# One exponential fill moved from the long attention visit to the short one

## The chip, the cores and the metric

The kernel runs on one core of a Trainium2 chip. The metric is the device time of one execution in microseconds, the median of several runs; lower is better.

## The reference

The reference adds an attention with a compressive memory and a gated feed-forward network, each weighted by a gate that is computed from the input. Cut to what matters:

```python
B, S, D, H, N, F = 1, 2048, 640, 32, 4, 1728      # Dh = 20, L = S // N = 512
g = sigmoid((x * gate_w).sum(-1, keepdims=True))
q, k, v = (x @ wq, x @ wk, x @ wv)                # as (B, H, N, L, Dh)
for s in range(N):                                # segments of 512 rows
    logits = einsum("bhqd,bhkd->bhqk", qs, ks) * Dh ** -0.5 + causal_mask
    a_dot = softmax(logits) @ vs
    a_mem = (phi(qs) @ M) / (phi(qs) @ z + 1e-6)  # phi(t) = t + 1 if t > 0 else exp(t)
    outs.append(sigmoid(beta) * a_mem + (1 - sigmoid(beta)) * a_dot)
    M, z = M + phi(ks).T @ vs, z + phi(ks).sum(0)
a = concat(outs) @ wo
b = (silu(x @ w1) * (x @ w3)) @ w2
return g * a + (1 - g) * b
```

## The kernel before

The work has two strands that share the tensor engine. The dense strand holds the products with 128x128 weight blocks: the projections (tiles `q`, `k`, `v`), the feed-forward network (`g` and `u` up, `f` down) and the output projection (`op`). Each of these is a *fill*: 9 or 15 matmuls of 512 columns (5 for the last down group) that add up in one PSUM bank, which one or two operations on VectorE or ScalarE then read out. The attention strand works on *quads* of four heads of one segment; there are 32 heads in 4 segments, so 32 quads.

A quad needs five `s` fills, five `t` fills and one `o` fill. An `s` fill computes scores by rows for two heads, one bank each, and VectorE reduces them to row maxima (line L641: one reduction, and one read of its accumulator into tile `m`, for every block of 128 query rows). A `t` fill computes transposed scores with the maxima already subtracted, again one bank for each of two heads; ScalarE turns them into exponentials in tile `P` (L673), GpSimd zeroes the masked part (L677). The `o` fill multiplies `P` of all four heads with the values into one bank, which VectorE copies to tile `oq` (L691). Two heads stand in the upper and lower 64 rows of the tensor engine, so their matmuls run side by side.

The eight PSUM banks are given out in the order of a queue. `bank_tile` takes the bank at the head. A small tile (`s`, `t`, `o`, `rr`, `nd`, ...) goes back to the tail at once, so the next user of that bank comes eight tiles later and waits for its readers. A dense fill is `held`: its bank is out of the queue until `filled()` at its last matmul.

The order on the tensor engine is the order in which the code is run (`manual_schedule` for that engine); the other engines' orders are the framework's. The main loop runs two generators. `attention()` goes through rounds `m`, each of 40 slots `n`, and issues the attention work; `step` issues a few dense matmuls (three, mostly) and adds to a counter, `clock["step"]`. In every slot the dense strand is run for as long as its share of the time lasts. In round `m` two slots carry a *visit*, a row of attention fills without a dense matmul in between. The long one (`BIG`, slot 5) has the fills 0, 2 and 1 of `s` for quad `m`, four `t` fills for quad `m - 1` and the `o` fill for quad `m - 2`. The short one (`SMALL`, slot 17) has `s` fills 3 and 4 and `t` fill 4. Before a visit the loop takes up to four or eight more dense steps until a condition holds: the long visit wants no fill held, that is a place between two dense fills; the short one ("amid") wants the held fill to have come far enough, and stands in its midst.

After the short visit, `max_rows` prepares the maxima for the next round and `load_pair` fetches queries and keys by DMA from GpSimd's queue in slots 12 and 18.

Of the kernel before, what the change touches and what calls it, by code (L numbers as in the profile page):

```python
# [18 lines left out]
S, D, H, DH, NSEG, L = 2048, 640, 32, 20, 4, 512  # L19
# [6 lines left out]
BIG = -1.0e38  # L26
# [12 lines left out]
def gated_mix(ctx: ExitStack, tc: tile.TileContext, xT, wqk, wv, w13, w2, w2h, wo, beta, out):  # L39
# [60 lines left out]


    here = tc.keep_in_program_order
    last = {}

    def split(dst, src, lo=None, pin=lambda ins: ins):
        pin(nc.scalar.copy(dst[:, 0], src))  # L106
# [2 lines left out]
    free, held = list(range(NB)), {}  # L109

    def bank_tile(name, hold=None):


        k = free.pop(0)
        ps = pp.tile([P, L], F32, tag=f"b{k}", name=name, bufs=1)
        if hold:
            held[k] = -hold
        else:
            free.append(k)
        return ps  # L120
# [6 lines left out]
    def split_psum(dst, src, name, pin=lambda ins: ins):  # L127

        hi = bank_tile(name)[:, :src.shape[-1]]
        pin(nc.scalar.copy(dst[:, 0], src))  # L130
        nc.scalar.copy(hi, dst[:, 0].bitcast(F32))
        nc.vector.tensor_sub(dst[:, 1], src, hi)
# [7 lines left out]
    def big_tile(name, dt=F32):  # L140
        return sp.tile([P, 4 * H * VE], dt, tag="big", name=name, bufs=1)

    def f_tile(name):
        return sp.tile([P, L], F32, tag="f", name=name, bufs=4)
# [7 lines left out]
    early, raws, clock = [], [], dict(step=0, oldest=0, next=0)  # L152
# [114 lines left out]
    late, stored = [], set()  # L267

    def store_later(dst, src, key=None, queue=nc.sync, n=4):
        late.append([n, dst, src, key, queue])  # L270
# [67 lines left out]
    def memory_read(c):  # L338
        pq = big.pop(("q", c))[:, :KB * L].rearrange("p (b n) -> p b n", b=KB)
        for qb in range(4):  # L340
            for hf in range(2):
                gm = f_tile(f"gm{c}_{qb}_{hf}")[:, :320]
                ps = bank_tile(f"nd{c}_{qb}_{hf}")
                nd = ps[:, :16 * VE].rearrange("p (h e) -> p h e", e=VE)
                todo = []
                for b in range(KB):
                    a0, a1 = HEADS[b]
                    u0, u1 = max(a0, 16 * hf), min(a1, 16 * hf + 15)
                    if u0 <= u1:
                        todo.append((b, a0, u0, u1))  # L350
                for n, (b, a0, u0, u1) in enumerate(todo):
                    nc.tensor.matmul(nd[:, u0 - 16 * hf:u1 - 16 * hf + 1, :],  # L352
                                     pq[:, b, qb * P:(qb + 1) * P],
                                     Ms[c - 1, b][:, u0 - a0:u1 - a0 + 1, :],
                                     start=n == 0, stop=n == len(todo) - 1, skip_group_check=True)
                r = sp.tile([P, 16], F32, tag="r16", name="nd_r")
                nc.vector.scalar_tensor_tensor(r, nd[:, :, DH], 1e-6, gH[:, 16 * hf:16 * hf + 16], op0=ALU.add, op1=ALU.mult)
                nc.vector.reciprocal(r, r)
                nc.vector.scalar_tensor_tensor(
                    gm.rearrange("p (h e) -> p h e", e=DH), nd[:, :, :DH], gate[:, c, 1, qb:qb + 1],  # L360
                    r.unsqueeze(2).broadcast_to([P, 16, DH]), op0=ALU.mult, op1=ALU.mult)
                store_later(gd[c][:, qb, 320 * hf:320 * hf + 320], gm, ("g", c, qb), n=2)
                yield 700
# [102 lines left out]
    def job_read(c):  # L466
        return 5.6, memory_read(c)
# [5 lines left out]
    def job_q(cs, mb, alloc={}):  # L473
        i = w_add(wqk[mb], D)
        return [(3.5, q_block(c, mb, i, alloc.get(c))) for c in cs]
# [206 lines left out]
    def pv_quad(p):  # L682

        ps = bank_tile(f"o{p}")
        for kb, (o, n) in enumerate(PSEG):
            for i in range(4):
                nc.tensor.matmul(ps[32 * i:32 * i + 32, kb * P:], heads[2 * p + i]["v"][:, kb],  # L687
                                 pairs[p + i // 2]["P"][:, i % 2, o:o + n],
                                 start=kb == 0, stop=kb == 3, skip_group_check=True)
        ot = sp.tile([P, L], F32, tag="oq", name=f"oq{p}", bufs=1)  # L690
        nc.vector.tensor_copy(ot, ps)  # L691
        c, h = heads[2 * p]["c"], heads[2 * p]["h"]
        nc.sync.dma_start(od[c][h:h + 4].rearrange("h e n -> (h e) n"), ot)
        q = p // 2 % 8
        for b in OUT.get(q, ()):
            after(8, o_load, c, b)
        if q == 7:
            after(6 if c < NSEG - 1 else 2, o_sums, c)
# [54 lines left out]
    def normalize(c):  # L753

        assert c in turned
        if not c:
            gms[c] = big_tile(f"oT{c}", FR)[:, :KB * L].rearrange("p (b n) -> p b n", b=KB)
        for b in range(KB):
            o, hi = f_tile(f"on{c}_{b}"), gms[c][:, b]
            ps = bank_tile(f"rr{c}_{b}")  # L760
            nc.tensor.matmul(ps, sel[:, b * P:(b + 1) * P], rR, start=True, stop=True)
            nc.vector.tensor_mul(o, oall[c][:, b].bitcast(F32), ps)
            if c:
                pt = bank_tile(f"gt{c}_{b}")
                for qb in range(4):
                    nc.tensor.transpose(pt[:, qb * P:(qb + 1) * P], hi[:, qb * P:(qb + 1) * P].bitcast(F32), ident)
                nc.vector.tensor_add(o, o, pt)  # L767
            nc.scalar.copy(hi, o)
            nc.vector.tensor_sub(oall[c][:, b], o, hi.bitcast(F32))
            yield 700  # L770
# [5 lines left out]
    def after(n, f, *a):  # L776
        soon.append([n, f, a])

    def tick():
        for e in list(soon):  # L780
            e[0] -= 1
            if e[0] <= 0:
                soon.remove(e)
                e[1](*e[2])

    NQUAD = NJ // 4


    BIG, SMALL = 5, 17
    VISITS = {BIG: (("s", 0, 0), ("t", 1, 0), ("t", 1, 1), ("o", 2), ("t", 1, 3), ("s", 0, 2), ("t", 1, 2), ("s", 0, 1)),  # L790
              SMALL: (("s", 0, 3), ("t", 1, 4), ("s", 0, 4))}

    def attention():

        for m in range(-1, NQUAD + 2):
            for n in range(40):
                if m == -1 and n < 40 - LEAD:
                    continue

                todo = VISITS.get(n, ()) if m != 1 else {BIG: VISITS[BIG][:3], BIG + 6: VISITS[BIG][4:]}.get(n, VISITS.get(n, ()))  # L800
                todo = [(kind, m - q, f) for kind, q, *f in todo if 0 <= m - q < NQUAD]
                if todo:
                    yield "amid" if len(todo) < 4 else "between"
                    for kind, q, f in todo:
                        if kind == "o":
                            pv_quad(2 * q)
                        else:
                            (s_fill if kind == "s" else t_fill)(q, *f)
                    if n == SMALL and 0 <= m < NQUAD:
                        after(4, max_rows, 2 * m)  # L810
                elif n in ((24, 36) if m < 0 else (BIG + 7, SMALL + 1)) and m + 1 < NQUAD:
                    load_pair(2 * (m + 1) + (n > BIG + 7 if m >= 0 else n > 24))
                tick()
                yield m
# [56 lines left out]
    def jobs_group(cs, g):  # L871
        return [job_up(cs, j) for j in GROUPS[g]] + [job_down(cs, g)]
# [51 lines left out]
    g = jobs_group(A, 0)  # L924
# [10 lines left out]
    q = job_q(B[:1], 0, {2: big_tile})  # L935
# [5 lines left out]
    q = job_q2(B, 3)  # L941
# [21 lines left out]
    for n, (_, g) in enumerate(head):  # L963
# [7 lines left out]
        elif n == 7:  # L971
            gates()
    stores(True)
    att = attention()

    def begin():
# [17 lines left out]
    while run:  # L994
        if slots == run[0] * 10 + LEAD:
            while step(run) is not None:
                pass
            stores(True)
            run = begin() if segs else None
            continue  # L1000
        place = next(att, None)
        if isinstance(place, str):

            for _ in range(4 if place == "amid" else 8):
                if (max(held.values(), default=-1) >= 0) if place == "amid" else not held:
                    break
                d = step(run)
                if d is None:
                    break
                credit -= d  # L1010
            next(att)
        slots += 1
        credit += run[2]
        while credit > 0:
            d = step(run)
            if d is None:
                if not segs:
                    break
                stores(True)
                run = begin()  # L1020
                continue
            credit -= d
# [57 lines left out]
```

## Time and profile before

| | |
|---|---|
| time, median of 3 runs | 1105.5 us (1105.04 to 1106.06) |
| the profiled execution's own time | 1107.73 us |
| its span from the first to the last instruction | 1105.9 us |
| TensorE busy | 1095.5 us (99%), granted clock 1.000 |
| VectorE busy | 598.1 us (54%) |
| ScalarE busy | 381.1 us (34%) |
| GpSimd busy | 584.3 us (53%) |
| HBM traffic | 137 GB/s over the span |

The page of the profile lists each engine's busy time, the chain of work that ended last, and the costliest groups of instructions by line. In the timeline a row holds the start, the length, the engine and line, the operation, the tiles written and read, and how many alike were merged; in square brackets stands the engine's idle time before it and what ended it. PE is the tensor engine, DVE VectorE, ACT ScalarE, POOL GpSimd. Matmuls overlap, so the tensor engine's pace is read from start to start and not from the length of one.

### The profile page before, as it was taken

The numbers are of one execution on the slowest core, as the hardware profiler recorded it, in microseconds if no ns is written. First come the engines' busy times: TensorE is split into PE (matmuls) and PEld (weight loads), VectorE is DVE, ScalarE is ACT, GpSimd is POOL, SyncE is SP. The second block draws the span as 40 slices with busy tenths as digits, with TensorE's granted clock in tenths as the row PEclk, the third lists the DMA queues.
The fourth block names the chain that finished last, engine by engine and source line by source line (L and its number), as shares of the span: only waits on it lengthen the run. The fifth ranks groups of instructions, "written<-read, shape, count | busy, mean of one in ns | idle before, by whom it ended". The sixth has DMA issues, their size and how long they took to land.

```text
span 1105.9 us, 17890 instructions
## 1 busy us (share of the span) xinstructions
PE 1095.5 (99%) x6290; PEld 853.9 (77%) x6290; DVE 598.1 (54%) x1711; ACT 381.1 (34%) x826; POOL 584.3 (53%) x729
## 2 busy tenths in 40 slices
PE   9999999999999999999999999999999999999998
PEld 6988877777777777777977777777777777777787
DVE  5032474355555564467153678875557765551575
ACT  6244233434233222145244543325334332223020
POOL 4155546466366363565075447556764655555263
PEclk9999999999999999999999999999999999999999
DMA  8356943334265232635358867355664342532122
GB/s 299 112 203 220 284 128 76 94 90 106 56 167 124 60 84 93 156 85 185 116 185 277 285 216 184 100 160 143 155 155 110 92 115 75 130 103 89 52 79 95
DMA packets 87545, 153.20 MB, mean 139 GB/s; under 512 B 11584, under 2 KB 25184, under 8 KB 87456
## 3 DMA queue, kind: packets, MB, share of 16 engines
q1 hardware_dynamic: 63040, 106.30, 30.3%
q0 software_dynamic: 20384, 38.68, 15.6%
q10 hardware_dynamic: 4032, 7.08, 1.8%
q8 instruction: 50, 0.82, 0.3%
q14 instruction: 39, 0.32, 0.1%
HBM read 96.56 MB, written 54.54 MB: 137 GB/s over the span
## 4 chain that ended last, share of the span: by engine, by line
PE 91%; DVE 4%; DMA 2%; ACT 1%; POOL 1%; issue 1%; ACTq 0%; SPq 0%; DVEq 0%; POOLq 0%
PE f L580 16%; PE g L257 16%; PE u L257 15%; PE k L257 6%; PE v L385 6%; PE op L837 6%; PE o L687 6%; PE q L257 5%; PE s L634 5%; PE t L667 4%; PE nd L352 1%; PE pm L449 1%; PE q L327 1%; DVE junk L641 1%; PE pkt L434 1%
## 5 line engine op out<-in xcount | busy, mean ns | idle before, releaser
L641 DVE CUSTOM_DVE_ANT_0 junk<-s,mask 128x256 bf16<-128x256 f32 (+3 forms) x512 | 250.4, 489 | 105.9 <-PE s L634 73.6
L673 ACT ACTIVATE P<-t 128x512 f32<-128x512 f32 (+1 forms) x384 | 172.5, 536 | 190.9 <-PE t L667 153.7
L257 PE MATMUL g<-X,W 128*128 128x512 f32 x840 | 208.5, 398 | 0.0
L179 POOL TENSOR_TENSOR W<-wr,W 128x640 fp32r<-128x640 f32 (+1 forms) x126 | 199.3, 1587 | 2.6
L174 POOL CAST W<-wr 128x640 fp32r<-128x640 f32 (+1 forms) x126 | 91.8, 733 | 199.5 <-PE f L580 46.2
L257 PE MATMUL u<-X,W 128*128 128x512 f32 x780 | 196.7, 399 | 0.0
L580 PE MATMUL f<-ht,W 128*128 128x512 f32 (+1 forms) x825 | 196.5, 395 | 0.0
L677 POOL TENSOR_SCALAR_AFFINE_SELECT P<-P 128x256 f32<-128x256 f32 x192 | 94.6, 502 | 180.1 <-ACT P L673 179.9
L257 PEld LDWEIGHTS g<-X,W 128*128 128x128 f32 x840 | 155.9, 188 | 36.7 <-issue 0.4
L580 PEld LDWEIGHTS f<-ht,W 128*128 128x128 f32 x825 | 153.0, 188 | 36.4 <-POOL W L179 0.2
L257 PEld LDWEIGHTS u<-X,W 128*128 128x128 f32 x780 | 144.0, 188 | 34.5 <-ACT P L673 0.3
L107 POOL TENSOR_TENSOR ht<-ft,ht 128x512 fp32r<-128x512 f32 x52 | 67.2, 1292 | 94.6 <-ACT ht L106 93.9
L611 POOL DMA_DIRECT2D qk<-qkd x128 | 83.5, 654 | 0.3
L634 PE MATMUL s<-qk 60*128 60x256 f32 (+3 forms) x512 | 78.7, 346 | 1.4 <-DVE fu L520 1.0
L257 PE MATMUL k<-X,W 128*128 128x512 f32 x300 | 77.0, 403 | 0.0
L687 PE MATMUL o<-P,vg 128*32 128x512 f32 (+3 forms) x1024 | 75.6, 435 | 1.4 <-DVE on L767 1.4
L519 ACT ACTIVATE ft<-g 128x512 f32<-128x512 f32 x52 | 31.2, 599 | 125.0 <-PE g L257 113.9
L520 DVE SCALAR_TENSOR_TENSOR fu<-ft,g 128x512 f32<-128x512 f32 x52 | 35.7, 686 | 67.8 <-ACT ft L519 58.2
L385 PE MATMUL v<-W,X 128*128 128x320 f32 (+1 forms) x480 | 71.9, 311 | 0.4 <-ACT P L673 0.4
L385 PEld LDWEIGHTS v<-W,X 128*128 128x128 f32 x480 | 71.0, 189 | 1.1 <-ACT P L673 0.6
L106 ACT CAST ht<-ft 128x512 fp32r<-128x512 f32 x52 | 32.2, 619 | 111.1 <-DVE ft L528 111.0
L588 DVE TENSOR_TENSOR acc<-f,acc 128x512 f32<-128x512 f32 x65 | 44.7, 689 | 44.9 <-PE f L580 44.7
(123 smaller groups left out, 1205.4 us busy)
## 6 DMA issues: line engine op xcount, KB each, us to landing
qk<-qkd POOLq DMA_DIRECT2D x128, 240.0 KB, 4.1
wr<-in_w_dram SPq DMA_DIRECT2D x80, 320.0 KB
qkd<-qs SPq DMA_DIRECT2D x20, 512.0 KB
qkd<-ks SPq DMA_DIRECT2D x20, 512.0 KB
od<-oq SPq DMA_DIRECT2D x32, 256.0 KB
wr<-in_wo_dram SPq DMA_DIRECT2D x20, 320.0 KB
vg<-vd SPq DMA_DIRECT2D x16, 336.0 KB
xr<-in_xT_dram SPq DMA_DIRECT2D x20, 256.0 KB
```

Of the source, the lines that this page charges most:

```text
L107: (lo or nc.gpsimd.tensor_sub)(dst[:, 1], src, dst[:, 0].bitcast(F32))
L174: hi = nc.gpsimd.tensor_copy(w[:, 0, :n], raw[:, :n])
L179: last["low"] = nc.gpsimd.tensor_sub(w[:, 1, :n], raw[:, :n], w[:, 0, :n].bitcast(F32))
L257: nc.tensor.matmul(ps, w[:, a, kb * P:(kb + 1) * P], x[:, b, kb, :], start=n == 0, stop=n == 14)
L385: nc.tensor.matmul(ps[:, :n1 - n0], x[:, a, kb, lb * P:(lb + 1) * P], wvt[kb][:, b, n0:n1], start=n == 0, stop=n == 14)
L580: nc.tensor.matmul(ps[:, :n1 - n0], w, h, start=n == 0, stop=n == len(ms) - 1)
L611: here(nc.gpsimd.dma_start(t[64 * i:64 * i + RH], qkd[c][RH * (h + i):RH * (h + i + 1)]))
L634: nc.tensor.matmul(ps[i][:, o:o + w], q[:, qb * P:(qb + 1) * P], key[:, :w], start=n == 0, stop=n == len(todo) - 1, skip_group_check=True)
L641: nc.vector.tensor_tensor_reduce(out=junk[:, :w], in0=ps[i][:, o:o + w], in1=mask[:, L - w:], scale=1.0, scalar=-3.0e38, op0=ALU.add, op1= ...
L673: last["exp"] = nc.scalar.activation(pairs[2 * m + k]["P"][:, i, o:o + n], ps[i][:, b:b + n], AF.Exp, scale=SCALE)
L677: nc.gpsimd.affine_select(d, d, pattern=[[0, 2], [0, n], [1, P]], base=0, channel_multiplier=-1, compare_op=ALU.is_ge, fill=0.0)
L687: nc.tensor.matmul(ps[32 * i:32 * i + 32, kb * P:], heads[2 * p + i]["v"][:, kb], pairs[p + i // 2]["P"][:, i % 2, o:o + n], start=kb == 0 ...
```

## The change

In the long visit, `t` fill 3 (written `("t", 1, 3)`: one quad back, fill 3) may be left out; the short visit then has four fills, and so takes all eight banks. This is done in a round where, at the long visit, the last dense fill was an up, down or output product (`PLAIN`, or `g`) and no small tile was issued in the last six steps. The short visit of such a round (`"four"`) is issued at the first slot from 8 on that lies between two dense fills, whose last fill was `u`, `f` or `op`, at least five steps after the long visit and more than two after the last small tile ("early"); if none has come by slot 17, up to four steps are taken to find one ("late"), and else it stands amid a held fill, with the `t` fill 3 ahead. `load_pair` keeps its slots.

```diff
-    last = {}
+    last = dict(small=0, visit=0)
...
     if hold:
         held[k] = -hold
+        last["dense"] = name[0]
...
+    PLAIN = "ufo"
     VISITS = {BIG: (("s", 0, 0), ("t", 1, 0), ("t", 1, 1), ("o", 2), ("t", 1, 3), ("s", 0, 2), ("t", 1, 2), ("s", 0, 1)),
-              SMALL: (("s", 0, 3), ("t", 1, 4), ("s", 0, 4))}
+              SMALL: (("s", 0, 3), ("t", 1, 4), ("s", 0, 4)),
+              "four": (("s", 0, 3), ("t", 1, 3), ("s", 0, 4), ("t", 1, 4))}
...
+                if n == SMALL or four and not done and 8 <= n < SMALL:
+                    if not done and 0 <= m <= NQUAD:
+                        yield "amid" if not four else "late" if n == SMALL else "early"
+                        if n == SMALL or last["go"]:
+                            fills = VISITS["four" if four else SMALL]
+                            visit(m, (fills[1],) + fills[:1] + fills[2:] if four and held else fills)
+                            done = True
+                            if m < NQUAD:
+                                after(4, max_rows, 2 * m)
+                elif n_fills:
+                    yield "amid" if n_fills < 4 else "between"
+                    if ("t", 1, 3) in todo and 0 < m <= NQUAD and last["dense"] in PLAIN + "g" and clock["step"] - last["small"] > 6:
+                        four = True
+                        todo = [t for t in todo if t != ("t", 1, 3)]
+                    visit(m, todo)
+                    last["visit"] = clock["step"]
...
+            def ready():
+                if place == "amid":
+                    return max(held.values(), default=-1) >= 0
+                if place == "between":
+                    return not held
+                return not held and last["dense"] in PLAIN and clock["step"] - last["visit"] >= 5 \
+                    and clock["step"] - last["small"] > 2
```

In the program as built, 22 of the rounds have a short visit with the moved fill: rounds 2 to 12, 18, 22 to 26 and 28 to 32. In rounds 4, 7 and 22 it stands amid a held fill; in round 32 there are no `s` fills left; in the other 18 it lies between two dense fills. The other rounds are as before.

The long visit on the tensor engine in round 6 of before, from the end of the `o` fill on (`t5_3_0` is `t` fill 3 of quad 5, first head; `s6_2` is `s` fill 2 of quad 6):

```order
L687 MATMUL o8_2797<-P9_2564,vg0_92 32x128 x2
L667 MATMUL t5_3_0_2817<-qk1_91 128x512
L667 MATMUL t5_3_1_2818<-qk1_91 128x512
L634 MATMUL s6_2_0_2825<-qk0_90 128x512
L634 MATMUL s6_2_1_2826<-qk0_90 128x512
L667 MATMUL t5_2_0_2833<-qk1_91 128x256
L667 MATMUL t5_2_1_2834<-qk1_91 128x256
```

The same place now:

```order
L691 MATMUL o8_2797<-P9_2574,vg0_92 32x128 x2
L638 MATMUL s6_2_0_2817<-qk0_90 128x512
L638 MATMUL s6_2_1_2818<-qk0_90 128x512
L671 MATMUL t5_2_0_2825<-qk1_91 128x256
L671 MATMUL t5_2_1_2826<-qk1_91 128x256
```

The `t` fill 3 is gone from behind the `o` fill, and the `s` fill 2 follows `o` at once.

The end of the short visit of that round on the tensor engine before, behind its `s` fill 3 (`f0_3_2` and `f0_3_3` are two dense fills of the same down group):

```order
L667 MATMUL t5_4_0_2909<-qk1_91 128x384
L667 MATMUL t5_4_1_2910<-qk1_91 128x384
L667 MATMUL t5_4_0_2909<-qk1_91 128x128
L667 MATMUL t5_4_1_2910<-qk1_91 128x128
L634 MATMUL s6_4_0_2919<-qk0_90 128x384
L634 MATMUL s6_4_1_2920<-qk0_90 128x384
L634 MATMUL s6_4_0_2919<-qk0_90 128x128
L634 MATMUL s6_4_1_2920<-qk0_90 128x128
L580 MATMUL f0_3_2_0_2888<-ht0_5_2701,W32_2607 128x512 x3
L580 MATMUL f0_3_3_0_2939<-ht0_3_2237,W30_2420 128x512 x3
```

And now, likewise behind `s` fill 3:

```order
L671 MATMUL t5_3_0_2906<-qk1_91 128x512
L671 MATMUL t5_3_1_2907<-qk1_91 128x512
L638 MATMUL s6_4_0_2913<-qk0_90 128x384
L638 MATMUL s6_4_1_2914<-qk0_90 128x384
L638 MATMUL s6_4_0_2913<-qk0_90 128x128
L638 MATMUL s6_4_1_2914<-qk0_90 128x128
L671 MATMUL t5_4_0_2927<-qk1_91 128x384
L671 MATMUL t5_4_1_2928<-qk1_91 128x384
L671 MATMUL t5_4_0_2927<-qk1_91 128x128
L671 MATMUL t5_4_1_2928<-qk1_91 128x128
L584 MATMUL f0_3_3_0_2939<-ht0_3_2237,W30_2373 128x512 x3
```

Before, the visit splits the fill `f0_3_2`, whose last three matmuls stand behind it. Now it stands between `f0_3_2` and `f0_3_3`, and a new fill, in need of a bank, comes right behind it.

On VectorE at that place, before:

```order
L588 TENSOR_TENSOR acc0_1953<-f0_3_1_0_2874,acc0_1953 128x512
L641 ISA junk_2901,m24_2621<-s6_3_0_2895,mask_89 128x256
L641 ISA m24_2621 128x1
L641 ISA junk_2903,m24_2621<-s6_3_0_2895,mask_89 128x256
L641 ISA m24_2621 128x1
L641 ISA junk_2905,m24_2621<-s6_3_1_2896,mask_89 128x256
```

And now:

```order
L592 TENSOR_TENSOR acc0_1953<-f0_3_1_0_2867,acc0_1953 128x512
L592 TENSOR_TENSOR acc0_1953<-f0_3_2_0_2881,acc0_1953 128x512
L645 ISA junk_2898,m24_2614<-s6_3_0_2892,mask_89 128x256
L645 ISA m24_2614 128x1
L645 ISA junk_2900,m24_2614<-s6_3_0_2892,mask_89 128x256
L645 ISA m24_2614 128x1
L645 ISA junk_2902,m24_2614<-s6_3_1_2893,mask_89 128x256
```

The sum that reads out the dense fill `f0_3_2` now stands ahead of the visit's reductions; before, that fill was not yet complete there. The lines L641 and L645 are the same line of the code.

More of the change, by code (lines that the diff above doesn't have):

```diff
@@ L129, in split_psum @@
         hi = bank_tile(name)[:, :src.shape[-1]]
+        if src.shape[-1] == L:
+            last["small"] = clock["step"]
         pin(nc.scalar.copy(dst[:, 0], src))
@@ L343, in memory_read @@
                 ps = bank_tile(f"nd{c}_{qb}_{hf}")
+                last["small"] = clock["step"]
                 nd = ps[:, :16 * VE].rearrange("p (h e) -> p h e", e=VE)
@@ L760, in normalize @@
             ps = bank_tile(f"rr{c}_{b}")
+            last["small"] = clock["step"]
             nc.tensor.matmul(ps, sel[:, b * P:(b + 1) * P], rR, start=True, stop=True)
@@ L789, in gated_mix, with visit @@
     BIG, SMALL = 5, 17
+    PLAIN = "ufo"
     VISITS = {BIG: (("s", 0, 0), ("t", 1, 0), ("t", 1, 1), ("o", 2), ("t", 1, 3), ("s", 0, 2), ("t", 1, 2), ("s", 0, 1)),
-              SMALL: (("s", 0, 3), ("t", 1, 4), ("s", 0, 4))}
+              SMALL: (("s", 0, 3), ("t", 1, 4), ("s", 0, 4)),
+              "four": (("s", 0, 3), ("t", 1, 3), ("s", 0, 4), ("t", 1, 4))}
     def attention():
+        def visit(m, todo):
+            for kind, q, *f in todo:
+                if 0 <= m - q < NQUAD:
+                    if kind == "o":
+                        pv_quad(2 * (m - q))
+                    else:
+                        (s_fill if kind == "s" else t_fill)(m - q, *f)
         for m in range(-1, NQUAD + 2):
+            four = done = False
             for n in range(40):
@@ L800, in attention @@
                 todo = VISITS.get(n, ()) if m != 1 else {BIG: VISITS[BIG][:3], BIG + 6: VISITS[BIG][4:]}.get(n, VISITS.get(n, ()))
[L801 to L811, printed above, removed]
+                n_fills = sum(0 <= m - q < NQUAD for _, q, *_ in todo)
+                if n == SMALL or four and not done and 8 <= n < SMALL:
[14 more added lines that the diff above has]
+                    last["visit"] = clock["step"]
+                if n in ((24, 36) if m < 0 else (BIG + 7, SMALL + 1)) and m + 1 < NQUAD:
                     load_pair(2 * (m + 1) + (n > BIG + 7 if m >= 0 else n > 24))
@@ L1002, in gated_mix @@
         if isinstance(place, str):
-            for _ in range(4 if place == "amid" else 8):
-                if (max(held.values(), default=-1) >= 0) if place == "amid" else not held:
+            def ready():
[5 more added lines that the diff above has]
+                    and clock["step"] - last["small"] > 2
+            last["go"] = ready()
+            for _ in range({"amid": 4, "late": 4, "early": 0}.get(place, 8)):
+                if ready():
                     break
```

## The prediction

> **What bounds the kernel now.** The page comes first: which engine is full, and what the end waits for.
>
> ```profile
> span 1105.9 us, 17890 instructions
> PE 1095.5 (99%) x6290; PEld 853.9 (77%) x6290; DVE 598.1 (54%) x1711; ACT 381.1 (34%) x826; POOL 584.3 (53%) x729
> ...
> PE 91%; DVE 4%; DMA 2%; ACT 1%; POOL 1%; issue 1%; ACTq 0%; SPq 0%; DVEq 0%; POOLq 0%
> ```
>
> TensorE is the bound: 99% busy, 91% of the chain that ended last. So only what lengthens or shortens the row of matmuls counts, and every gap in it is paid in full. The timeline shows one long visit, in round 6, from its first `s` fill to the next dense fill.
>
> ```profile
> 269.77 0.50 PE L634 MATMUL s<-qk 60*128 60x512 f32 x2
> ...
> 269.88 0.69 DVE L528 SCALAR_TENSOR_TENSOR ft<-fu,u 128x512 f32<-128x512 f32 x1 [2.05 <-PE u L257]
> ...
> 270.11 0.64 PE L667 MATMUL t<-qk 62*128 62x512 f32 x6
> 270.48 0.68 DVE L641 CUSTOM_DVE_ANT_0 junk<-s,mask 128x512 bf16<-128x512 f32 x1
> ...
> 270.68 2.36 PE L687 MATMUL o<-P,vg 128*32 128x512 f32 x32
> ...
> 272.97 0.50 PE L667 MATMUL t<-qk 62*128 62x512 f32 x2
> ...
> 273.11 0.69 DVE L691 COPY oq<-o 128x512 f32<-128x512 f32 x1 [1.08 <-PE o L687]
> ...
> 273.31 0.39 PE L634 MATMUL s<-qk 60*128 60x512 f32 x2
> ...
> 273.54 0.40 PE L667 MATMUL t<-qk 62*128 62x256 f32 x4
> 273.56 2.19 ACT L673 ACTIVATE P<-t 128x512 f32<-128x512 f32 x6 [0.45 <-PE t L667]
> ...
> 273.78 0.57 PE L634 MATMUL s<-qk 60*128 60x384 f32 x4
> ...
> 274.28 5.85 PE L580 MATMUL f<-ht,W 128*128 128x512 f32 x24
> ```
>
> From start to start, a fill in the middle of a visit takes 0.23 us (273.31 to 273.54), the first behind `o` 0.34 (272.97 to 273.31), the last with the way back to a dense fill 0.50 (273.78 to 274.28). The short visit of the same round:
>
> ```profile
> 280.05 0.51 PE L634 MATMUL s<-qk 60*128 60x256 f32 x4
> ...
> 280.40 0.40 PE L667 MATMUL t<-qk 62*128 62x384 f32 x4
> ...
> 280.60 0.42 DVE L641 CUSTOM_DVE_ANT_0 junk<-s,mask 128x256 bf16<-128x256 f32 x1 [1.13 <-PE s L634]
> 280.63 0.45 PE L634 MATMUL s<-qk 60*128 60x384 f32 x4
> ...
> 280.94 0.08 DVE L641 DVE_READ_ACCUMULATOR2_ANT m<- 128x1 f32 x1
> 281.01 13.45 PE L580 MATMUL f<-ht,W 128*128 128x512 f32 x57
> 281.06 0.42 DVE L641 CUSTOM_DVE_ANT_0 junk<-s,mask 128x256 bf16<-128x256 f32 x1
> 281.41 0.08 DVE L641 DVE_READ_ACCUMULATOR2_ANT m<- 128x1 f32 x1
> 281.64 0.42 DVE L641 CUSTOM_DVE_ANT_0 junk<-s,mask 128x256 bf16<-128x256 f32 x1
> ```
>
> It takes 0.96 us (280.05 to 281.01), and the matmuls go on while VectorE has hardly begun: the fill that follows is the held one and already has its bank. Other rounds look the same; in the chain, `o` and the dense piece behind the long visit are as far apart in round 2 as in round 31:
>
> ```profile
> 174.17 2.29 PE o L687 x32
> 177.77 3.67 PE u L257 x15
> ...
> 977.91 2.29 PE o L687 x32
> 981.51 3.66 PE u L257 x15
> ```
>
> 3.60 us both times. So before the change neither visit has much waiting in it to take away.
>
> **The change part by part.** I write V for the start of a visit's first fill.
>
> *Long visit, 21 rounds (round 32 apart).* The moved fill leaves. Behind `o` remain three fills: 0.34 for the first, 0.23, and the last with the way back. That last one took 0.50, where the short visit's last, of the same 384 and 128 columns, took 0.38 (280.63 to 281.01). The difference of 0.12 is a bank: counted from the queue, the long visit uses 2+2+2+1+2+2+2+2 = 15 banks, so the second head of `s` fill 1 gets the bank that `o` had, and VectorE's copy of it ends at 273.11 + 0.69 = 273.80, after that fill began (273.78). With 13 banks it gets one of `t` fill 1, long read out. So 274.28 - 272.97 = 1.31 becomes 0.34 + 0.23 + 0.38 = 0.95: **-0.36** a round, and at least -0.23 if the 0.12 has another cause.
>
> *Short visit, 17 rounds between two dense fills.* The matmuls alone would need 0.34 + 0.23 + 0.23 + 0.38 = 1.18 instead of 0.96. But the visit takes all eight banks, the first for `s` fill 3, and the next dense fill gets the ninth place in the queue, which is that first bank again. It is free when VectorE has made both reductions of that head. In front of them in VectorE's order stands the read-out of the dense fill that has just ended. Rows for it: in the long visit above, which also lies between dense fills, that read-out starts at V + 0.11 and takes 0.69, and the first reduction starts at 270.48, V + 0.71. From the first reduction of a bank to the end of its second accumulator read: 281.41 + 0.08 - 280.60 = 0.89. So the bank is free at V + 1.60. How fast TensorE follows VectorE, the one eight-bank visit of the old kernel shows, in round 1, where the eighth bank was that of a `g` fill:
>
> ```profile
> 154.68 0.33 PE L634 MATMUL s<-qk 60*128 60x384 f32 x1
> ...
> 155.25 0.69 DVE L520 SCALAR_TENSOR_TENSOR fu<-ft,g 128x512 f32<-128x512 f32 x1
> 155.99 0.50 PE L634 MATMUL s<-qk 60*128 60x384 f32 x3 [0.98 <-DVE fu L520]
> ```
>
> 155.99 - 155.94 = 0.05. So the dense fill starts at V + 1.65 instead of V + 0.96: **+0.69**. That is 0.22 for the moved fill and 0.47 of waiting. The eighth bank, that of the dense fill read out at V + 0.80, delays the last `t` fill by about 0.1 us at most, and the longer wait covers that.
>
> The two reductions are the price that decides. Their rows give 0.89 us for 512 columns. [...]
>
> Bounds of the short visit: if nothing stood ahead of the reductions, they would start as in the old short visit, V + 0.55 (280.60), and the fill at V + 1.49: +0.53. I take +0.69, since the order shows the read-out ahead. Round 3 is the exception: its down group is the first, read out by ScalarE, so +0.53.
>
> *Short visit, rounds 4, 7 and 22, amid a held fill.* Seven banks are left, so the eighth (second head of `t` fill 4) is that of the first head of `t` fill 3, which now comes first. ScalarE began such a fill 0.59 us after its start (273.56 against 272.97); with 0.6 us for it and 0.05, the last half fill starts at about V + 1.24 and needs the 0.43 that lie between the delayed head at 273.85 (273.80 + 0.05) and 274.28: V + 1.67, +0.71, near the others. Bounds: +0.22 without a wait, and +1.3 with one more operation of 0.6 us ahead on ScalarE.
>
> *Round 10.* Behind the visit comes a small `rr` matmul, which takes the first bank; the dense fill needs the second, whose reductions start 281.64 - 280.60 = 1.04 us later. The `rr` matmul covers some 0.4 of it:
>
> ```profile
> L761 PE MATMUL rr<-rR,sel 96*128 96x512 bf16 x20 | 7.8, 391 | 0.0
> ```
>
> So +0.6 more. *Round 32* moves a fill between two visits without reductions: 0.
>
> *What else moves.* Two exponentials and a mask step go with the fill, some 10 us later at most; their reader, the `o` fill, comes with the next long visit but sits there behind those of `t` fill 4, which stood in the short visit before too. `max_rows` and its two small DMAs come earlier, which hurts nothing. GpSimd's queue and its loads of queries and keys keep their slots, behind the short visit as before. The rest of the visit's banks come free while the first dense fill behind it runs.
>
> *Sum.* 17 x (0.69 - 0.36) = 5.6; round 3: 0.53 - 0.36 = 0.2; three held ones: 3 x 0.35 = 1.1; round 10: 0.6. Together **+7.5 us**. Against the profiled execution's own 1107.73 us (span 1105.9) that is 1115.2; that execution lies 2.2 above the median of 1105.5, and on the median's scale the sum gives **1113.0 us**.
>
> **The rivals.**
>
> *The drain is hidden, and the kernel is faster.* If the next dense fill's bank were free by V + 1.18, the waits of the short visit would be gone, and the long one's saving left: 21 x (0.22 - 0.36) = -2.9, 1102.6 us. The point of decision is V + 1.32 (0.96 + 0.36): a fill that starts earlier than that gains. For it: VectorE is only 54% busy. Against it: even without a read-out ahead the rows give V + 1.49. Chance 0.07.
>
> *The wait is there but short, and all cancels.* For this the fill would have to start at that point, V + 1.32; less 0.05 and 0.71, the pair of reductions would have 0.56 us instead of 0.89. Then 1105.5 us. The 0.46 from one reduction's start to the next in the same bank (280.60 to 281.06) speak against it. Chance 0.04. [...]
>
> *More stands ahead.* If VectorE had a second dense product to make ahead of the reductions in each of the 18 rounds (as `fu` and then `ft`), each would cost 0.69 - 0.09 = 0.60 more, with the overlap of 0.09 seen at 270.48: +10.8, some 1124 us; a share of it where other dense work falls on VectorE then. Against it: a fill of 15 matmuls takes 3.67 us (the row at 177.77), in which `fu`, 0.69, is made. Chance 0.09.
>
> That the change does nothing is excluded by the order of instructions in 22 rounds.
>
> **How the numbers follow.** My forecast has 0.80. Its own bounds: +3.2 if nothing stands ahead of the reductions and the held visits wait for nothing (18 x 0.17 - 3 x 0.14 + 0.6), and +11.9 if the long visit gives back 0.23 alone and ScalarE is late (17 x 0.46 + 0.3 + 3 x 1.07 + 0.6): 1108.7 to 1117.4. These hold nearly all of the 0.80; to hold 8 in 10, the range goes a little further, into the dearer case: 1108.5 to 1118. About 0.2%, 2.2 us, is what a measurement of this kernel can tell from no change. Faster by more than that: 0.08, the hidden drain; within it: 0.04; slower: 0.88, the rest.
>
> **What would show it.** In the profile after, behind `o` comes `s`, and the dense fill 0.95 us later. In the short visits between dense fills, the row of the dense fill starts about 1.65 us after the visit's first `s`, with idle time of TensorE ahead of it put down to VectorE's `m` or `junk` on the reductions' line, about 0.47 us in each of 18 rounds, some 8 us in the list of waits; busy time and granted clock stay. I am wrong if that fill starts at V + 1.2, if the long visit's end is not 0.36 shorter, or if the time goes elsewhere, as into late loads of queries and keys.

## The result, and the profile after

The changed kernel takes 1118.06 us (median of 4 runs, 1116.8 to 1119.88), the kernel before 1105.78 us (median of 4 runs beside them): a ratio of 1.0105, 95% interval 1.0093 to 1.0117. It is slower, as forecast, by about 12 us instead of 7.5. That is the upper edge of the range, which ends at 1118: the ratio, put on the 1105.5 us from which the forecast started, gives 1117.1. The profiled execution took 1118.71 us. Its page:

```profile
span 1117.0 us, 17899 instructions
PE 1097.3 (98%) x6290; PEld 853.1 (76%) x6290; DVE 598.5 (54%) x1711; ACT 380.6 (34%) x826; POOL 583.8 (52%) x729
...
PE 92%; DVE 5%; issue 1%; DMA 1%; ACT 1%; SPq 0%; DVEq 0%
...
L260 PE MATMUL g<-X,W 128*128 128x512 f32 x840 | 209.9, 401 | 7.6 <-DVE m L645 7.6
...
L584 PE MATMUL f<-ht,W 128*128 128x512 f32 (+1 forms) x825 | 196.6, 395 | 2.8 <-DVE m L645 2.8
```

The same matmuls, 1.8 us more of busy time in a span that is 11.1 us longer. New are the idle times ahead of dense groups, ended by `m`, the reads of the maxima's accumulator. (All lines of the attention code have moved down by four, L641 to L645 and so on.) The long visit of round 6, and then the short one, in the timeline:

```profile
272.16 2.36 PE L691 MATMUL o<-P,vg 128*32 128x512 f32 x32
...
274.45 0.50 PE L638 MATMUL s<-qk 60*128 60x512 f32 x2
...
274.79 0.40 PE L671 MATMUL t<-qk 62*128 62x256 f32 x4
...
275.03 0.41 PE L638 MATMUL s<-qk 60*128 60x384 f32 x4
...
275.37 1.89 PE L584 MATMUL f<-ht,W 128*128 128x512 f32 x7
...
281.81 0.50 PE L638 MATMUL s<-qk 60*128 60x256 f32 x4
281.92 0.69 DVE L592 TENSOR_TENSOR acc<-f,acc 128x512 f32<-128x512 f32 x1 [1.39 <-PE f L584]
...
282.52 0.41 DVE L645 CUSTOM_DVE_ANT_0 junk<-s,mask 128x256 bf16<-128x256 f32 x1
...
283.33 0.08 DVE L645 DVE_READ_ACCUMULATOR2_ANT m<- 128x1 f32 x1
...
283.47 2.83 PE L584 MATMUL f<-ht,W 128*128 128x512 f32 x11 [0.31 <-DVE m L645]
```

From the first fill behind `o` to the dense fill it is now 275.37 - 274.45 = 0.92 us, before 1.31. In the short visit VectorE first reads out the old dense fill (V + 0.11), starts the first reduction at V + 0.71, ends the second accumulator read at V + 1.60, and the dense fill starts 0.06 later, at V + 1.66. Not all visits look like this one. Round 29:

```profile
945.56 0.50 PE L638 MATMUL s<-qk 60*128 60x256 f32 x4
...
948.27 5.32 PE L260 MATMUL g<-X,W 128*128 128x512 f32 x15 [1.35 <-DVE m L645]
953.42 2.94 PE L260 MATMUL u<-X,W 128*128 128x512 f32 x12
```

Here the dense fill starts only at V + 2.71, and then takes 953.42 - 948.27 = 5.15 us for 15 matmuls; the same 15 behind the same wait take 3.58 in round 23 (804.67 to 808.25). On VectorE in the same stretch:

```profile
946.27 0.42 DVE L645 CUSTOM_DVE_ANT_0 junk<-s,mask 128x256 bf16<-128x256 f32 x1
...
947.09 0.08 DVE L645 DVE_READ_ACCUMULATOR2_ANT m<- 128x1 f32 x1
947.31 0.42 DVE L645 CUSTOM_DVE_ANT_0 junk<-s,mask 128x256 bf16<-128x256 f32 x1
...
948.13 0.08 DVE L645 DVE_READ_ACCUMULATOR2_ANT m<- 128x1 f32 x1
```

The first head was read out at 947.17, as priced; TensorE moved when the second head was, at 948.21. The slow fill behind the wait is the granted clock (the columns are the window, the busy time and count of PE, PEld, DVE, ACT and POOL, the granted clock, the DMA share and GB/s):

```profile
944.00:948.80 4.80, 3.44 (x24) 2.56 (x23) 2.77 (x10) 2.47 (x5) 3.11 (x4) 1.00 0.47 137
948.85:952.26 3.41, 3.41 (x10) 2.64 (x9) 2.21 (x13) 0.44 (x3) 3.39 (x7) 0.50 0.06 4
```

The list of TensorE's waits sums up what is new (total, times, longest), of after:

```profile
PE g L260 <- DVE m L645: 7.6, 10, 1.4
PE f L584 <- DVE m L645: 2.8, 6, 1.3
...
PE op L860 <- DVE m L645: 0.6, 2, 0.3
```

and in the same list of before there is one wait that after no longer has, in round 19:

```profile
PE o L687 <- DVE on L767: 1.4, 1, 1.4
```

The change of each visit's time between the two traces, from the start of the last matmul ahead of it to the start of the first dense matmul behind it (in round 10's short visit less 0.34 us for the small `rr` matmul that now stands between the two):

| visits | change, each | predicted | sum |
|---|---|---|---|
| short, 12 rounds between dense fills | +0.70 (0.69 to 0.75) | +0.69 | +8.5 |
| short, rounds 3; 18, 23, 24, 29 | +1.58; +1.75 | +0.53; +0.69 | +8.6 |
| short, rounds 4, 7, 22, amid a held fill | +0.65 | +0.71 | +2.0 |
| short, round 10 | +1.83 | +1.29 | +1.8 |
| long, 18 rounds | -0.40 (0.38 to 0.43) | -0.36 | -7.2 |
| long, rounds 10, 18, 30 | -0.77, -0.57, -1.06 | -0.36 | -2.4 |
| long, round 19 (no moved fill) | -1.48 | 0 | -1.5 |
| round 32, both | -0.01 | 0 | 0 |

That is +9.7 us. With 5.15 - 3.58 = 1.6 us for the fill at half clock it makes 11.3, against the span's 11.1.

### The profile page after: what moved, and what is told of

The parts are those of the page before. It is cut to its first block, busy times and chain, and to the rows that moved or that the text cites. A ratio compares the mean times of both kernels' runs of the same rounds, so it can differ in the third digit from the quotient of the medians.

```text
span 1117.0 us, 17899 instructions
## 1 busy us (share of the span) xinstructions
PE 1097.3 (98%) x6290; PEld 853.1 (76%) x6290; DVE 598.5 (54%) x1711; ACT 380.6 (34%) x826; POOL 583.8 (52%) x729
## 4 chain that ended last, share of the span: by engine, by line
PE 92%; DVE 5%; issue 1%; DMA 1%; ACT 1%; SPq 0%; DVEq 0%
PE g L260 18%; PE f L584 16%; PE u L260 16%; PE k L260 6%; PE op L860 6%; PE v L389 6%; PE o L691 6%; PE q L260 5%; PE s L638 4%; PE t L671 3%; DVE junk L645 3%; PE nd L356 1%; PE pm L453 1%; PE q L330 1%; PE gt L771 1%
## 5 line engine op out<-in xcount | busy, mean ns | idle before, releaser
L645 DVE CUSTOM_DVE_ANT_0 junk<-s,mask 128x256 bf16<-128x256 f32 (+3 forms) x512 | 249.9, 488 | 98.6 <-PE s L638 64.7
L260 PE MATMUL u<-X,W 128*128 128x512 f32 x780 | 194.4, 398 | 0.0
L681 POOL TENSOR_SCALAR_AFFINE_SELECT P<-P 128x256 f32<-128x256 f32 (+1 forms) x192 | 93.5, 496 | 175.1 <-ACT P L677 174.9
L638 PE MATMUL s<-qk 60*128 60x256 f32 (+3 forms) x512 | 75.1, 345 | 1.1 <-DVE fu L524 1.0
L532 DVE SCALAR_TENSOR_TENSOR ft<-fu,u 128x512 f32<-128x512 f32 x52 | 35.7, 687 | 60.4 <-PE u L260 59.8
```

What stands on the lines that cost most here:

```text
L260: nc.tensor.matmul(ps, w[:, a, kb * P:(kb + 1) * P], x[:, b, kb, :], start=n == 0, stop=n == 14)
L638: nc.tensor.matmul(ps[i][:, o:o + w], q[:, qb * P:(qb + 1) * P], key[:, :w], start=n == 0, stop=n == len(todo) - 1, skip_group_check=True)
L645: nc.vector.tensor_tensor_reduce(out=junk[:, :w], in0=ps[i][:, o:o + w], in1=mask[:, L - w:], scale=1.0, scalar=-3.0e38, op0=ALU.add, op1= ...
L681: nc.gpsimd.affine_select(d, d, pattern=[[0, 2], [0, n], [1, P]], base=0, channel_multiplier=-1, compare_op=ALU.is_ge, fill=0.0)
```

## The experiments

The theory after the result: the bank in ninth place sets the start of the next tile; in five rounds a small tile of `max_rows` (`nh`, by which the maxima are split and which TensorE never touches) took that place, so that the dense fill got the second head's bank, 1.05 us later. The rivals: VectorE was busier in those five rounds; the new place between two dense fills has a price of its own; the loss lies in moving the fill at all. In what follows, changes of a visit are against the trace of before, and each ratio is against runs of the kernel before on the same chip in the same series.

**1. Another bank in ninth place.** `t` fill 3 goes ahead in every four-fill visit, so that the first bank is one that ScalarE frees, and not VectorE.

```diff
-    visit(m, (fills[1],) + fills[:1] + fills[2:] if four and held else fills)
+    visit(m, (fills[1],) + fills[:1] + fills[2:] if four else fills)
```

> All four-fill visits begin with the t fill 3; nothing else differs from the changed kernel. Theory A (the queue of banks): the dense fill behind the visit waits for the bank it is given, the ninth in the queue. That is now the first head of t fill 3, which ScalarE reads: begun at V + 0.55, 0.6 us long, so the fill starts at about V + 1.2 to 1.3 instead of V + 1.65 (V is the start of the visit). In rounds 3, 18, 23, 24 and 29 the small tile of max_rows has taken that bank and the fill gets the second head's: V + 1.7 instead of V + 2.7. Together some 13 x 0.4 + 5 x 1.0 = 10 us less than the changed kernel, with no idle stretch long enough for the clock: 1105 to 1108 us. Rival B (the place: a visit between two fills costs by itself, whatever the banks): 1116 to 1118 us, as now. Rival C (VectorE has too much to do there): the same 1116 to 1118, since its work is the same.

Measured: 1111.04 us, ratio 1.0036 (1.0024 to 1.0049), above the 1105 to 1108 that were expected. The ordinary short visits fall from +0.70 to +0.32, the five of the small tile from +1.75 (1.58) to +0.70 to +0.79; the held ones, whose order is as before, stay at +0.65. Who releases the dense fill has changed with the bank:

```profile
PE g L260 <- ACT P L677: 1.3, 4, 0.3
...
PE f L584 <- ACT P L677: 0.5, 1, 0.5
```

So the wait belongs to the bank and its reader. The visits also show a new loss: round 30's long visit, +4.70, and at the head of the same list stands a wait for queries and keys:

```profile
PE s L638 <- DMA qk<-qkd: 2.9, 3, 1.9
```

**2. The small tile out of ninth place.** The matmul order is the same, word for word; only the maxima are split six slots later.

```diff
-    after(4, max_rows, 2 * m)
+    after(10 if four else 4, max_rows, 2 * m)
```

> max_rows comes ten slots instead of four behind a four-fill visit, so that its small tile cannot take a bank before the next dense fill does; the order on the tensor engine is the same. Theory A: in rounds 3, 18, 23, 24 and 29 the fill gets the first head's bank back and starts at V + 1.65 instead of V + 2.7: 5 x 1.05 = 5.2 us less, and no stretch of 1.5 us idle is left, so the granted clock is 1.000 in all runs (the drop to 0.5 for 3.4 us in the profile cost 1.6): 1111 to 1113 us. Rivals B and C: no change by this, 1116 to 1118 us.

Measured: 1118.01 us, ratio 1.0096 (1.0081 to 1.0112). The total missed what was expected, and still the visits answer: rounds 18, 23, 24 and 29 have +0.69 to +0.71 and round 3 has +0.54, 1.05 less each, 5.2 in all. The small tile was the cause. But round 30's long visit gave it all back, +5.01 where the changed kernel has -1.06:

```profile
PE g L260 <- DVE m L645: 3.5, 10, 0.7
PE s L638 <- DMA qk<-qkd: 2.8, 2, 2.3
PE f L584 <- DVE m L645: 1.8, 6, 0.3
```

The longest wait for `m` is now 0.7 instead of 1.4; a wait for the load of queries and keys has taken its place. From 956.70 to 963.50 the granted clock was 0.50, and that wait was over only at 957.73. The waits of the changed kernel had covered a late load: there the slowest of these loads took 6.1 us, but round 30's long visit began 15.6 us after round 29's short one (945.56 to 961.18) and did not wait for it; here it began after 13.6 us (941.39 to 954.96), and the load took 6.86.

**3. Both together.**

> Both edits: the t fill 3 first, and max_rows ten slots behind. Theory A: all 18 visits between fills end at about V + 1.2 to 1.3, a round costs 0.3 for the short visit and gives 0.40 back in the long one: about as the kernel before or a little faster, 1102 to 1106 us. Rivals B and C: 1112 to 1118 us.

Measured: 1109.81 us, ratio 1.0028 (1.0017 to 1.0039), above the 1102 to 1106 that were expected. The short visits between dense fills have +0.29 to +0.37, the held ones +0.65, round 10 +0.45; long ones -0.40; and round 30 again +3.91. Its loads and its visit in the timeline:

```profile
940.48 1.30 POOL L615 DMA_DIRECT2D qk<-qkd  x2
...
944.00 1.31 POOL L615 DMA_DIRECT2D qk<-qkd  x2
...
948.86 0.46 PE L638 MATMUL s<-qk 60*128 60x512 f32 x1 [0.76 <-DVE acc L592]
951.33 0.47 PE L638 MATMUL s<-qk 60*128 60x512 f32 x1 [2.01 <-DMA qk<-qkd]
...
952.20 4.05 PE L691 MATMUL o<-P,vg 128*32 128x512 f32 x32
```

and in the chain of waits the load that was waited for:

```profile
944.65 6.55 DMA qk<-qkd
```

It landed at 951.20; the median of such loads over the changed kernel's span is 4.2 us. The `o` fill behind it took 4.05 us instead of 2.36, and the mean granted clock of this execution was 0.998; in run 4, where the same fill took 4.05 us as well, the granted clock was 0.51 from 951.20 to 954.60. In this kernel the short visit of round 29 comes early, and only 11 us of dense work lie between it and round 30's long visit.

**4. The place alone.** `t` fill 3 stays in the long visit; the three-fill short visit moves to the place between two dense fills.

```diff
-    fills = VISITS["four" if four else SMALL]
-    visit(m, (fills[1],) + fills[:1] + fills[2:] if four and held else fills)
+    fills = VISITS[SMALL]
+    visit(m, fills)
...
-    todo = [t for t in todo if t != ("t", 1, 3)]
```

> The short visit stands between two dense fills as in the changed kernel, but t fill 3 stays in the long visit: three fills, six banks. Theory A: the next dense fill finds a bank that was free long before, so the visit takes 0.95 us as before, and the kernel 1103 to 1107 us. Rival B (the place itself costs): 18 x 0.7 = 12 us more, about 1118 us. Rival C: somewhat less than the changed kernel, 1112 to 1116, since VectorE has the same work in the same place.

Measured: 1108.97 us, ratio 1.0016 (1.0008 to 1.0025), above the 1103 to 1107 that were expected. No short visit changed, but for round 10, where the `rr` matmul now follows the visit, with -0.29: with six banks in use the next dense fill finds one free. The rival of the place's price falls. What is left of the loss is again round 30, +3.79; most of round 19's gain is here too (1.17), so that much comes from the place.

**5 and 6. Round 29 as before.** Runs 3 and 4, with the early visit of round 29 taken back.

```diff
-    if ("t", 1, 3) in todo and 0 < m <= NQUAD and last["dense"] in PLAIN + "g" and clock["step"] - last["small"] > 6:
+    if ("t", 1, 3) in todo and 0 < m <= NQUAD and m != 29 and last["dense"] in PLAIN + "g" and clock["step"] - last["small"] > 6:
```

> As in the run with both edits (t fill 3 ahead in every four-fill visit, row maxima six slots later), but round 29 stays as before the change: three fills at slot 17, t fill 3 in the long visit. Theory: an early short visit of round 29 leaves only 11 us of dense work until the long visit of round 30, less than GpSimd's queue and the DMA engines need for that visit's queries and keys. With round 29 back, round 30's long visit loses its 3.9 us and the drop of the granted clock behind it (1.7 us in most executions): visits sum to +2.6 - 0.33 + 0.38 - 3.9 - 0.4 = -1.6 us, so 1105.0 (1104 to 1106.5), granted clock 1.0. Rival, that the late load belongs to the load itself and moves on to another round, or that the clock falls whatever round 29 does: 1108 to 1110, a clock of 0.996 to 0.998 as in the run with both edits.

> The new place alone (t fill 3 stays in the long visit, three-fill short visits move between two dense fills), round 29 as before the change. Theory: the place alone costs nothing but round 29's late load; without it the visits sum to +2.2 - 3.8 = -1.6 us: 1105.0 (1104 to 1106.5), clock 1.0, level with the run above within 0.6 us, since moving t fill 3 gains 0.40 and costs 0.32 per round when it stands first. Rival: the place has a price of its own that the late load hid, 1107 to 1110.

Measured, run 3 without round 29: 1108.38 us, ratio 1.0008 (0.9996 to 1.0019); run 4 without it: 1106.04 us, ratio 0.9987 (0.9976 to 0.9998). Round 30's long visit falls from +3.91 and +3.79 to +0.60 in both, so round 29's early visit was behind most of the late load. The waits of run 3 without round 29:

```profile
PE s L638 <- DMA qk<-qkd: 1.2, 1, 1.2
```

The visits sum to -0.2 and -0.95, not to -1.6: round 30 still waits about half a microsecond longer than in the kernel before, and rounds 13, 16 and 23 vary. The median of the first is above what was expected: 7 of its 12 runs had a mean granted clock of 0.996 to 0.998, against 2 of 11 in the second. The executions with at least 0.999 lie at 1105.5 to 1107.6 in the one and 1104.2 to 1106.8 in the other. Why the clock fell more often there is open. The second beats the kernel before by about 0.1% (its interval ends just below 1), and does so without moving any fill.

**7. The fill alone.** `t` fill 3 moves, but every short visit stays in slot 17, amid a held fill.

```diff
-    if n == SMALL or four and not done and 8 <= n < SMALL:
+    if n == SMALL:
...
-    yield "amid" if not four else "late" if n == SMALL else "early"
+    yield "amid"
```

> The other half of the change alone: t fill 3 moves into the short visit, but every short visit stays at slot 17 amid a held dense fill, as rounds 4, 7 and 22 have it in the changed kernel (t fill 3 ahead). Theory of the queue of banks: each of some 21 rounds then costs what rounds 4, 7 and 22 cost, +0.65 in the short visit and -0.40 in the long one: 21 x 0.25 = +5.3 us, 1112 (1110.5 to 1113.5); no visit with +1.75, since the row maxima's tile comes behind the held fill, and a clock of 0.999 to 1.0. Rival, that only the place between two dense fills makes an eight-bank visit wait: the short visit costs nothing amid a held fill and the long ones keep their gain, 1106.7 - 8.4 = 1098.

Measured: 1113.01 us, ratio 1.0061 (1.0047 to 1.0074). All 21 short visits have +0.64 to +0.71, 18 of their long ones -0.40. In neither of the two places is an eight-bank visit free. Amid a held fill the wait lies inside the visit:

```profile
279.15 0.51 PE L671 MATMUL t<-qk 62*128 62x512 f32 x2
279.50 0.64 PE L638 MATMUL s<-qk 60*128 60x256 f32 x8
...
279.98 0.86 PE L671 MATMUL t<-qk 62*128 62x384 f32 x4
280.34 0.29 PEld L671 LDWEIGHTS t<-qk 62*128 62x128 f32 x3 [0.24 <-ACT P L677]
...
280.77 0.50 PE L584 MATMUL f<-ht,W 128*128 128x512 f32 x1
```

The last `t` fill, which needs the bank of the first, takes 0.79 us from start to start (280.77 - 279.98) instead of 0.46 in run 3 (280.84 - 280.38, where the visit had all eight banks). Its weight loads wait for ScalarE's `P`, the read-out of that bank.

**8. The dose.** The small tile is taken at once, so that it has the ninth place in all 18 visits between dense fills.

```diff
-    after(4, max_rows, 2 * m)
+    after(1, max_rows, 2 * m)
```

> The changed kernel with the row maxima's small tile taken one slot behind the visit instead of four, so that it has the ninth place in the queue in all 18 visits between dense fills, not in five. Theory: 13 more visits make the next dense fill wait for the second head of s fill 3, +1.05 us each: 13 x 1.05 = +13.7 less a little for round 10, where a wait of 0.8 stands already: 1131 (1128 to 1134) from 1118, with a short visit of +1.75 in each of them; more if the clock falls after more of these waits. Rival, that the five visits waited long because of what stood on VectorE there and not because of the small tile: 1118 (1117 to 1121).

Measured: 1135.47 us, ratio 1.0253 (1.0234 to 1.0272); against the changed kernel's 1.0105, some +16 us. Of the 18, 17 have +1.73 to +1.84 and round 3 +1.58: 12 visits more, by 1.04 each, and with +0.60 in round 17 the short visits' sum rises by 13.1 us; round 10 is unchanged. The rival of a busier VectorE falls. The total lies above the 1131 that was expected; in the trace stand, beside the visits priced, round 13's long one with +2.80 and a mean granted clock of 0.995: the 15 matmuls of the dense fill behind round 10's visit took 403.81 - 398.57 = 5.24 us, those of the next such fill 407.52 - 403.86 = 3.66.

```profile
PE g L260 <- DVE m L645: 12.2, 9, 1.4
PE f L584 <- DVE m L645: 8.0, 6, 1.4
PE op L860 <- DVE m L645: 2.7, 2, 1.4
PE rr L766 <- DVE m L645: 1.4, 1, 1.4
```

**9. The kernel as it was priced.** Run 2 without round 29: the ninth place goes to the dense fill in every visit between dense fills, and round 30's load is no longer pressed by an early visit.

> The changed kernel with both disturbances taken out that the prediction did not have: the row maxima's small tile six slots later in four-fill visits (so that the next dense fill takes the ninth place in every visit between dense fills), and round 29 as before the change (no late load in round 30). It is thus the kernel that the prediction priced, in one round less. Theory: every short visit between dense fills +0.70, none +1.75, long visits -0.40, round 30's long visit about +0.6; by the visits of the run with the maxima later, +15.81 - 0.71 in the short ones and -4.55 - 5.01 + 0.39 + 0.60 in the long ones, +6.5 us together: 1.0059 of the kernel before, 1113.2 (1112 to 1115). Rival, that the time of the changed kernel above this lies in neither of the two: 1116 to 1119, as the change itself.

Measured: 1112.67 us, ratio 1.0057 (1.0043 to 1.0071), the visits together +5.9 us; the profiled execution ran at a clock of 1.0. Every short visit between dense fills has +0.69 to +0.75, but for round 3 (+0.54) and round 10 (+1.83).

```profile
PE g L260 <- DVE m L645: 3.2, 9, 0.7
PE f L584 <- DVE m L645: 1.8, 6, 0.3
...
PE s L638 <- DMA qk<-qkd: 1.1, 1, 1.1
```

Round 30 still waits 1.1 us for its load. Otherwise that is the kernel that the prediction's sum described, in one round less, for which the sum gives 7.2 us: with the two disturbances out, most of what the forecast lacked is gone. That the totals come so close is in part cancelling: round 30 (+0.49 for -0.36) and round 10 are dearer than priced, round 19 (-1.48) is cheaper.

## Why the prediction was right, and where its sum fell short

- *TensorE is the bound, and every gap is paid in full*: held. 9.7 us in the visits and 1.6 at the lower clock account for the 11 us of the span.
- *Long visit, -0.36*: -0.40. The last fill with the way back takes 0.34 (275.03 to 275.37) and not the 0.38 borrowed from the short visit. In run 4, where the long visit keeps its 15 banks, it still takes 0.51 (955.87 to 956.38), as the reading of the bank would have it.
- *Short visit between dense fills, +0.69*: +0.70 in 12 rounds, and each step of it stands in the timeline at the time given: read-out at V + 0.11, first reduction at V + 0.71, bank free at V + 1.60, TensorE 0.06 behind. The two reductions with their reads take 0.89 us again (282.52 to 283.41).
- *Rounds 4, 7 and 22, +0.71*: +0.65, and run 7 showed the same in 21 rounds. *Round 3, +0.53*: +0.54 once the small tile was out of the way (runs 2 and 9). *Round 10*: +1.83 instead of +1.29. VectorE was still at the reductions of the long visit, which lies only 3.8 us back there; so the read-out of the dense fill starts at V + 0.53 instead of V + 0.11, and all behind it 0.42 later:

```profile
390.83 0.50 PE L638 MATMUL s<-qk 60*128 60x256 f32 x4
...
391.14 0.29 DVE L645 CUSTOM_DVE_ANT_0 junk<-s,mask 128x128 bf16<-128x128 f32 x1
...
391.36 0.68 DVE L532 SCALAR_TENSOR_TENSOR ft<-fu,u 128x512 f32<-128x512 f32 x1
...
391.96 0.42 DVE L645 CUSTOM_DVE_ANT_0 junk<-s,mask 128x256 bf16<-128x256 f32 x1
...
392.90 0.38 PE L766 MATMUL rr<-rR,sel 96*128 96x512 bf16 x1 [0.31 <-DVE m L645]
```

- **The term that was mis-sized** is "the next dense fill gets the ninth place in the queue". It was made 17 times at 0.69 and once at 0.53; in five of these rounds the place had gone to the small tile of `max_rows`, and the term was 1.05 larger: +5.2 us, removed by run 2, repeated in 12 more rounds by run 8. The prediction said that an earlier `max_rows` "hurts nothing"; it looked at its two DMAs, not at its bank.
- *Missed on the other side*: four long visits came out shorter than the sum has them. Round 19 lost the wait of 1.4 us for `on`; in run 4 the new place alone gives 1.17 there. Round 30 gained 0.7 more than others: its two first heads stood 0.68 us apart in the kernel before, behind a load, and stand together in the changed one. Round 18's 0.2 lies ahead of its `o` fill, which began 1.08 us after the visit's first `s` before and begins 0.89 after it now. Round 10's 0.4 lies behind its visit, where the dense fill behind the `rr` matmul starts 0.04 us after it instead of 0.42. What held the two back before is not shown.

```profile
950.10 0.50 PE L634 MATMUL s<-qk 60*128 60x512 f32 x1
...
950.78 0.47 PE L634 MATMUL s<-qk 60*128 60x512 f32 x1 [0.19 <-DMA qk<-qkd]
```

- *Busy time and granted clock stay*: wrong for the clock. Its fall cost 1.6 us in the profiled execution; 2 of the 4 runs have a mean granted clock of 0.998, the other two 1.000.
- *On the median's scale*: the profiled execution of before lay 2.2 us above the median the forecast started from, that of after only 0.65 above its own: the two executions differ by 11.0 us, the medians by 12.3. No row says where that microsecond lies.
- *The number*: the mechanism and its price held in most rounds, but that the time still came out at the end of the range is partly luck. Against the sum's 7.5 us the visits have 5.2 more from the small tile and 0.5 from round 10, and some 3.7 less from the long visits and the held ones; the clock's 1.6 came on top.
- The rivals: hidden drain, and all cancels: fell. *More stands ahead of the reductions*: a second dense product ahead did not come, and the 12 ordinary rounds show none of it. More time did come, 1.05 us in each of five rounds, since the release there waits for the second head's reductions; and in round 10 other reductions did stand ahead.
- *It would be wrong if the time goes into late loads*: in the changed kernel it did not, since its own waits covered the load. In runs 1 to 4 it did. The prediction looked at the loads' slots, and not at the time from round 29's short visit to the load's use.

## What to carry to other kernels

When a stretch of the critical engine uses as many buffers as a rotation has, follow the queue one place further, tile by tile, and count the tiles that this engine never touches: whoever takes the next place decides whose read-out is waited for (here +0.32, +0.70 or +1.75 us a visit). Repairing one wait on the critical engine can uncover a transfer that the wait had covered (in run 2, 5.2 us repaired and a wait of 2.3 us for a load uncovered), so judge a repair by the place it was made for as well as by the total. And test a composite change in its parts: here the place between two dense fills was worth about 0.1% by itself, and the fill that was moved there cost all of it and more.

## What the runs showed of the hardware that was not expected

- A single wait of 1.35 us on TensorE can be followed by a lower granted clock. In round 29 of the changed kernel the clock fell to 0.50 at 948.85, 0.58 us after TensorE had gone on, for 3.41 us; rounds 18, 23 and 24 had the same wait and no such fall. In run 8, with 18 waits of 24.3 us in all, the mean granted clock was 0.995, and matmuls were slow at three places: behind waits of 1.35 us at 398.57 (the fill of 5.24 us) and at 443.96 (two `op` matmuls in 1.05 us instead of 0.62), and at 526.05 (two `s` matmuls in 1.06 us instead of 0.50). In run 2 the granted clock was 0.50 from 956.70 to 963.50, from before the end of a wait of 2.3 us for a load (957.73); the profiled execution of run 1, with a wait of 1.9 us for a load, had a mean granted clock of 0.996. That of run 9, whose longest new wait was 1.1 us, had 1.0. The kernel before is not free of it: in one series 5 of its 23 runs had a mean granted clock of 0.997 or 0.998. How long a wait has to be for a fall, and why equal waits differ, is not shown.
- A load of queries and keys, 4.2 us at the median from issue to landing in the changed kernel, took 6.55 us in round 29 of run 3, where the DMA queues also carried weights (five transfers of 320 KB between 930 and 962).
